# Loading k and v as bf16 by the transfer itself, from GpSimd's queue, in an attention and squared-ReLU kernel on one Trainium2 core

## The chip, the core and the metric

The kernel runs on one core of a Trainium2 chip. A core has TensorE (PE, matrix products), VectorE (DVE), ScalarE (ACT), GpSimd (POOL) and SyncE (SP, which here only issues transfers), and 16 DMA engines that all transfers share. A transfer is issued by an engine's instruction stream: in this kernel SP, POOL and, in three places at the start and one at the end, ACT. Each stream is worked off in its own order, so an instruction that waits holds up what stands behind it on that engine.

The metric is the time of one execution on the device in microseconds (us), median of several runs. A profiled execution gives the trace; its span is the time from the first to the last instruction that the profile shows.

## The reference

Eight batches of eight heads, 576 tokens, head size 64, and 16 extra "beacon" keys and values that every token sees. Causal attention, then a two-layer product with a squared ReLU:

```python
k_all = np.concatenate([beacon_k, k], axis=2)
v_all = np.concatenate([beacon_v, v], axis=2)
scores = scale * np.matmul(q, k_all.transpose(0, 1, 3, 2))
causal[:, Nb:] = np.triu(np.ones((S, S), dtype=bool), k=1)
scores = np.where(causal, -1000000000.0, scores)
a = np.exp(scores - scores.max(-1, keepdims=True))
a /= a.sum(-1, keepdims=True) + 1e-09
attn = np.matmul(a, v_all)
x = np.ascontiguousarray(attn.transpose(0, 2, 1, 3)).reshape(B * S, H * D)   # 4608 x 512
h = x @ w_in                                                                  # 4608 x 2048
r = np.maximum(h, 0.0)
out = (r * r) @ w_out                                                         # 4608 x 512
```

All inputs and the output are float32 in device memory (HBM); the kernel's matrix products take bf16.

## The kernel before

**Attention.** The 592 keys of a batch (16 beacon, 576 own) are cut into five tiles of 128 rows, the last of 80. Scores are made transposed, keys on the partitions, queries along the row: a matmul takes 64 rows of `kT` (one head) as weights and streams `qT` (line 709). ACT takes the exponential into `pt` (line 817), DVE masks the diagonal (839), PE multiplies with `vb` (861), whose 65th column of ones gives the sum of the row, and DVE divides into `xn` (879, 881). `xn` is transposed into `xT`, by PE for batches 0 to 2 (line 930) and by DMA transposes from SP for the later ones (line 913).

**The product layers.** Tokens go in nine chunks of 512. The first layer (line 1174, for the last two chunks 1048) leaves its result in PSUM, ACT or DVE apply ReLU and square (1190 to 1202), and the second layer (1225 for the first chunk, 1288 for the others) multiplies with `w_out`, in a form with seven products in place of eight that needs sums on DVE (`sum_area`, line 1259). `osb` goes to the output.

**How q, k and v come in.** For batches 0 and 1, q and k are loaded in a strided form and transposed by PE (lines 527 and 596, then 559 and 562). From batch 2 on, k and q are loaded by SP, in float32, into one of six staging buffers `stg` (`add_load`, lines 434 to 439), POOL casts each to bf16 in `qk_area` (line 391), and when all five tiles of k, or the five parts of q, are there, SP issues a DMA transpose into `kT` (line 472) or two into `qT` (479, 482). v goes the same way into `vb`, without a transpose; for batches 0 and 1 POOL issues v's loads, after that SP. A k or v tile is eight pieces of 64 float32 (256 bytes) per row, one for each head, and tile 0 has a small extra transfer for the beacons. q is packed, so that a partition reads four tokens (1 KB) at once, but for the first 64 tokens of each head. `kb`, the bf16 form of k in `qk_area`, lies by head pairs, then tiles; so does `kT`.

A load needs a free staging buffer, and the buffer comes free with the cast. There are two copies each of `kb`, `qb`, `kT`, `qT` and `vb`, used by batches in turn: the cast of k waits until the transpose of batch b-2 is done, the cast of v until the attention of b-2 is. v's loads stand behind the issue of the same batch's transposes (`behind`, line 1389).

**What sets the order.** All instructions are registered as operations with an engine, an estimated duration, a priority, dependencies and buffers taken and given back; the class `Order` plays them through once when the program is built, and each engine's instructions are emitted in the order that comes out. `NUDGE` adds to the priorities of single operations, `HOME` fixes the engine where two are possible. `behind` keeps an issue order, `sync` makes an operation wait for another's end though it needs no data from it. Transfers of one issuing engine use eight semaphores in turn: a transfer's issue waits for the eighth one before it to land.

The weights are loaded by POOL, cast to bf16 on the way (`w_in` line 956, `w_out` line 964), in four parts each; SP's first load for batch 2 waits for the last part of `w_out` (`sync`, line 1385).

Of the kernel before, what the change touches and what calls it, by code (L numbers as in the profile page):

```python
# [17 lines left out]
    "tp0.0.0k": 303.651, "ek0.0.2": 3.595, "eq0.0.2": -114.892, "tp0.0.3q": -625.983, "tp0.1.0q": -1223.21,  # L18
    "tp0.1.1k": -824.389, "tp0.1.1q": -1236.66, "tp0.1.3q": -293.65, "qk0.1.2": 199.004, "qk1.0.0": 617.234,
    "av1.0.0": 1322.97, "qk1.1.1": -99.218, "qk3.1.1": 160.424, "tpb1": 1048.34, "tp1.0.1q": -111.345,  # L20
    "av4.0.0": 99785.9, "qk5.7": 99599.4, "exp5.7.0.0.0": 0.67, "qk7.13": 99392, "exp7.13.1.0.0": -47.842,
    "av7.0.0": 100066.370, "xtp1.0.0": 100463.971, "sq0.1.0": 208.303, "s1.0.2.1": 120.167, "s1.0.11.1": 336.481,
    "s1.0.5.1": 124.485, "s1.0.6.0": 71.868, "s1.0.13.0": 41.267, "s2.0.0.0": 56.582, "s2.0.1.0": -99691.1,
    "s2.0.1.2": -20.164, "st0": 41.41, "s2.0.2.1": 690.82, "s2.0.3.0": -109.423, "s2.0.3.1": -11.019,
    "s1.1.0.0": 44.191, "s1.1.8.0": 172.315, "sq1.4.0": -18.208, "s1.1.11.0": 265.496, "s1.1.6.0": 21.125,
    "s1.1.7.0": 229.509, "relu1.7.0": -405.788, "s1.1.14.0": 202.878, "s1.1.15.0": 500.257, "relu1.15.0": 61.707,
    "sum1.3.0": 1108.42, "ev1.u2.None": -82.041, "s2.1.5.1": -100238.506, "s2.1.4.1": -100250.303, "st2": 71.853,
    "tr2q": -203.512, "ld2v1": 28.104, "qk8.2": 100211.101, "exp8.2.1.0.0": -71.878, "qk9.7": 100144.007,
    "exp9.7.-1.0.0": 613.641, "exp9.7.-1.1.0": -8.39, "exp9.7.1.1.3": 182.463, "av9.0.0": 100352.010,
    "exp10.10.-1.1.0": -136.856, "exp10.10.0.0.0": -77.132, "exp10.10.1.0.0": -81.198, "mask10.0.0": -1407.66,  # L30
    "mask10.0.1": -100.11, "mask10.0.2": -199.111, "av10.0.1": 100284.953, "xte2.0.0": 0.336, "xtp2.0.2": 1453.06,
    "sq2.0.0": -147.071, "s1.2.3.0": -101055.411, "relu2.8.0": 93.279, "s1.2.10.0": -63.379, "s1.2.11.0": 583.95,
    "s1.2.4.0": -101060.421, "s1.2.5.0": -289.582, "s1.2.6.0": 23.584, "s1.2.7.0": 55.54, "s1.2.13.0": 20.328,
    "s2.2.2.0": -79.04, "s2.2.2.1": 66.099, "s2.2.6.1": -100314.663, "ev2.u2.None": 280.652, "ev2.c21.None": 433.942,
    "tr3qh": 97.18, "qk12.2": 100532.120, "av12.0.0": 101401.751, "av13.0.1": 101286.864, "exp14.11.1.0.0": 42.246,
    "av14.0.0": 100786.006, "xt3.0": -3.244, "xt3.1": -8.867, "xt3.3": 359.559, "xt3.4": 141.761,
    "s1.3.0.0": -101287.044, "s1.3.2.0": -88.641, "s1.3.8.0": -144.116, "s1.3.9.0": -101292.034, "s1.3.11.0": 912.185,
    "s1.3.5.0": 197.731, "relu3.5.0": -0.786, "s1.3.6.0": -20.095, "sq3.6.0": -5.491, "relu3.15.0": 57.142,
    "sum3.1.1": 1346.77, "s2.3.1.1": 105.485, "ev3.c1.None": 2252.87, "s2.3.5.0": 207.684, "s2.3.7.1": -101083.342,
    "s2.3.4.1": 115.307, "exp16.5.0.0.0": -133.173, "av18.0.0": 101606.833, "av19.0.0": 101753.541,  # L40
    "norm19.0.1": -1613.43, "xt4.0": 111.84, "xt4.3": 195.866, "xt4.4": 195.876, "s1.4.0.0": 931.962,
    "s1.4.1.0": 29.835, "s1.4.2.0": 11.266, "relu4.8.0": 45.602, "s1.4.9.0": -999.566, "sq4.4.0": 10.238,
    "s1.4.11.0": 91.505, "s1.4.6.0": 1005.57, "s1.4.12.0": -942.138, "s2.4.1.0": -12.509, "s2.4.4.0": 1155.18,
    "ld5k1": 217.137, "tr5q": -230.794, "exp20.5.0.0.0": 50.236, "qk21.8": -389.395, "exp21.8.-1.1.0": -59.523,
    "av21.0.0": 101166.223, "av21.0.1": -102.59, "exp22.11.1.0.0": 116.231, "xt5.0": 65.062, "xt5.2": 165.327,
    "xt5.3": 165.337, "s1.5.0.0": 118.705, "relu5.0.0": 45.886, "sq5.0.0": 21.556, "s1.5.2.0": -102472.597,
    "s1.5.3.0": -102569.183, "sq5.1.0": -113.507, "s1.5.8.0": -102706.946, "s1.5.10.0": -907.562,
    "s1.5.11.0": -908.572, "s1.5.4.0": -918, "relu5.4.0": -222.554, "s1.5.5.0": -4.327, "s1.5.6.0": -102580.170,
    "s1.5.7.0": -51.547, "s1.5.12.0": -7.182, "relu5.12.0": -140.259, "sq5.6.0": -436.745, "s2.5.1.0": -83.039,
    "s2.5.2.0": -117.659, "s2.5.5.0": 380.959, "ev5.u3.None": 40.167, "s2.5.4.1": 916.305, "ld6k0": 39.806,  # L50
# [25 lines left out]
    "relu5.12.0": "ACT", "sq5.6.0": "DVE", "ev5.u3.None": "ACT", "sq6.1.0": "ACT", "sq6.5.0": "ACT",  # L76
    "relu6.15.0": "ACT", "ev6.c1.None": "ACT", "ev6.c21.None": "ACT", "h7.0.c1": "ACT", "sq7.0.01": "ACT",
    "sq7.0.10": "ACT", "relu7.1.10": "ACT", "sq8.0.00": "ACT", "sq8.0.10": "ACT", "sq8.0.11": "ACT", "h8.1.u3": "ACT",
    "relu8.1.10": "DVE",
}  # L80


# [168 lines left out]
def kernel(  # L251
# [11 lines left out]
    nc = tc.nc  # L263
    B, H, S, D = q.shape
# [1181 lines left out]
```

## Time and profile before

| | |
|---|---|
| median of 3 runs | 330.49 us (328.14 to 330.75) |
| the profiled execution | 331.13 us, of which its span is 329.4 us |
| mean granted TensorE clock of it | 0.993 |
| HBM read, written | 37.22 MB, 9.44 MB |
| packets of all queues | 125827, of which 106586 under 512 bytes |

The busiest groups of the engines beside PE: the exponentials on ACT (line 817) 71.2 and 23.3 us, ReLU on ACT (1190) 45.6, the masks on DVE (839) 36.9, and on POOL the casts of q and k (391, `qk_area<-stg`) 40.9 us for 60 of them and of v (`vb<-stg`) 28.6 us for 38.

How to read it: a page of the profile gives busy time, share of the span and number of instructions by engine; then the span in 40 slices of 8.2 us, each digit the busy share in tenths, with the clock that the throttle granted TensorE and the busy share of the DMA engines (where packets overlap in time, this share can pass 1 in a stretch). A line of a group reads: source line, engine, operation, written tile <- read tile, count | busy us, mean ns of one | idle time of the engine before them and what ended it. A line of a wait reads: who, for whom: us in total, times, longest. In a table of windows each engine has its busy time and (xinstructions), in the order PE, PEld (weight loads), DVE, ACT, POOL, then the granted clock, the DMA share and GB/s, which count the bytes as written. "SPq" is SP issuing a transfer, "landing" the end of a transfer counted from its issue. Queue 1 is what SP issues, queue 0 what POOL issues, queue 10 what ACT issues.

### The profile page before, as it was taken

The page shows a single profiled execution, that of the slowest core. Times are in us where ns is not written, and L with a number is a line of the kernel's source. Part 1 is how long each engine was busy: PE and PEld are TensorE (multiplying, and loading weights), DVE is VectorE, ACT ScalarE, POOL GpSimd, SP SyncE. Part 2 cuts the span into 40 slices and gives each one's busy share as a digit, 9 for nine tenths or more (in the row PEclk, how much of TensorE's full clock was granted, in tenths as well). Part 3 has the DMA queues.
Part 4 walks back from the last instruction along what each step waited for, and adds up shares of the span by engine and source line. Part 5 has one row for each costly group of instructions (what it writes and reads, how often), then busy time and mean ns, then how long its engine had stood idle before and what let it go on. Part 6 is the DMA issues. An engine that isn't in the chain of part 4 may idle for free.

```text
span 329.4 us, 8951 instructions
## 1 busy us (share of the span) xinstructions
PE 312.8 (95%) x3660; PEld 233.1 (71%) x3678; DVE 237.9 (72%) x490; ACT 235.5 (71%) x352; POOL 101.0 (31%) x147
## 2 busy tenths in 40 slices
PE   2999999989999999999799999999999999999995
PEld 1578865645786468888577545775788788888884
DVE  3888765847985877586937768577955698896871
ACT  3896977469757886787664868688777664879831
POOL 9935703404704614223234105620220260000000
PEclk9999999999999999999799999999999999999999
DMA  9999998999999999499979959987900240020032
GB/s 169 219 207 218 205 152 227 138 254 209 207 198 227 266 181 224 107 236 155 200 177 202 252 95 191 250 164 140 200 5 0 57 146 0 19 112 1 31 130 98
DMA packets 125827, 51.61 MB, mean 157 GB/s; under 512 B 106586, under 2 KB 120794, under 8 KB 125786
## 3 DMA queue, kind: packets, MB, share of 16 engines
q1 hardware_dynamic: 116125, 41.92, 58.5%
q0 software_dynamic: 8512, 8.49, 15.2%
q10 hardware_dynamic: 1149, 0.62, 0.8%
q8 instruction: 29, 0.48, 0.6%
q14 instruction: 12, 0.10, 0.1%
HBM read 37.22 MB, written 9.44 MB: 142 GB/s over the span
## 4 chain that ended last, share of the span: by engine, by line
PE 56%; DMA 21%; DVE 7%; SPq 6%; POOL 5%; ACT 3%; issue 2%; POOLq 0%; DVEq 0%
PE ps L1288 22%; PE ps L1174 15%; PE ps L861 6%; DMA qk_area<-in_q_dram 5%; DMA stg<-in_k_dram 4%; DMA w_out<-in_moe_w_out_dram 4%; PE strip L1048 3%; PE strip L709 3%; DVE sum_area L1259 3%; PE ps L1048 3%; DMA stg<-in_q_dram 3%; SPq L439 2%; PE strip L1288 2%; DMA w_in<-in_moe_w_in_dram 2%; DMA kT<-qk_area 2%
## 5 line engine op out<-in xcount | busy, mean ns | idle before, releaser
L1174 PE MATMUL ps<-xT,w_in 128*128 128x512 bf16 (+6 forms) x626 | 104.7, 314 | 0.7
L817 ACT ACTIVATE pt<-strip 128x1024 bf16<-128x1024 f32 (+3 forms) x89 | 71.2, 851 | 18.3 <-PE strip L709 11.1
L1174 PEld LDWEIGHTS <-w_in 128*128 128x128 bf16 x640 | 57.2, 98 | 34.2 <-issue 1.4
L1190 ACT ACTIVATE g<-ps 128x512 bf16<-128x512 f32 (+2 forms) x85 | 45.6, 539 | 23.3 <-PE ps L1174 22.1
L391 POOL CAST qk_area<-stg 128x512 bf16<-128x512 f32 (+2 forms) x60 | 40.9, 693 | 52.5 <-DMA stg<-in_k_dram 35.3
L1288 PEld LDWEIGHTS <-g 128*128 128x128 bf16 x512 | 48.9, 99 | 8.9 <-issue 2.0
L391 POOL CAST vb<-stg 128x512 bf16<-128x512 f32 (+1 forms) x38 | 28.6, 766 | 84.2 <-DMA stg<-in_v_dram 47.5
L839 DVE TENSOR_TENSOR pt<-pt,tri 128x512 bf16<-128x512 bf16 (+1 forms) x93 | 36.9, 421 | 15.4 <-ACT pt L817 15.1
L1288 PE MATMUL ps<-w_out,g 128*128 128x256 bf16 x352 | 45.9, 277 | 0.0
L1288 PEld LDWEIGHTS <-sum_area 128*128 128x128 bf16 x384 | 36.3, 98 | 7.2 <-DVE sum_area L1259 1.6
L861 PEld LDWEIGHTS <-pt 128*128 128x128 bf16 x930 | 34.9, 98 | 6.6 <-issue 1.0
L861 PE MATMUL ps<-vb,pt 128*128 128x65 bf16 x930 | 37.9, 194 | 0.2
L1192 DVE TENSOR_SCALAR g<-ps 128x512 bf16<-128x512 f32 (+2 forms) x43 | 27.1, 630 | 9.5 <-PE ps L1174 8.2
L881 DVE TENSOR_TENSOR xn<-ps,rcp 128x320 bf16<-128x320 f32 (+2 forms) x64 | 31.5, 492 | 2.4 <-DVE rcp L879 0.2
L1288 PE MATMUL ps<-w_sum,sum_area 128*128 128x256 bf16 x240 | 30.9, 273 | 1.2 <-DVE sum_area L1259 1.0
L709 PEld LDWEIGHTS <-kT 64*128 64x128 bf16 x666 | 21.1, 96 | 15.2 <-issue 8.0
L1200 ACT ACTIVATE g<-g 128x1024 bf16<-128x1024 bf16 (+2 forms) x30 | 29.4, 983 | 1.9 <-DVE g L1192 1.3
L709 PE MATMUL strip<-qT,kT 64*128 64x64 bf16 (+14 forms) x548 | 29.3, 238 | 1.3 <-DMA kT<-qk_area 0.8
L1202 DVE TENSOR_TENSOR g<-g 128x1024 bf16<-128x1024 bf16 (+2 forms) x34 | 22.1, 652 | 11.3 <-ACT g L1190 10.9
L817 ACT ACTIVATE pt<-ps 128x512 bf16<-128x512 f32 x42 | 23.3, 599 | 9.1 <-PE ps L709 5.1
L879 DVE RECIPROCAL rcp<-ps 128x5 f32<-128x5 f32 (+2 forms) x64 | 12.1, 190 | 19.0 <-PE ps L861 17.9
L1312 DVE TENSOR_TENSOR osb<-ps,osb 128x512 f32<-128x512 f32 (+1 forms) x26 | 16.8, 647 | 12.2 <-PE ps L1288 6.4
(91 smaller groups left out, 366.3 us busy)
## 6 DMA issues: line engine op xcount, KB each, us to landing
out_dram<-osb SPq DMA_DIRECT2D x16, 512.0 KB, 3.5
stg<-in_q_dram SPq DMA_DIRECT2D x24, 256.0 KB, 4.5
stg<-in_k_dram SPq DMA_DIRECT2D x18, 256.0 KB, 5.3
stg<-in_v_dram SPq DMA_DIRECT2D x18, 256.0 KB, 5.0
w_in<-in_moe_w_in_dram POOLq DMA_DIRECT2D x4, 512.0 KB, 11.5
w_out<-in_moe_w_out_dram POOLq DMA_DIRECT2D x4, 512.0 KB, 11.2
stg<-in_v_dram POOLq DMA_DIRECT2D x6, 256.0 KB, 8.0
stg<-in_k_dram SPq DMA_DIRECT2D x6, 224.0 KB, 3.8
```

The costliest lines, as they stand in the source:

```text
L391: eng[e].tensor_copy(dst, src)
L709: nc.tensor.matmul(st[hj][:, at + lo:at + hi], kT[b % 2][64 * hj:64 * hj + 64, pr, 128 * c:128 * c + 128], rhs, start=True, stop=True)
L817: nc.scalar.activation(out, in_, AF.Exp, bias=0.0, scale=scale)
L839: nc.vector.tensor_tensor(out=d, in0=d, in1=tri[0:rows, m0:m0 + m, 0:w][:, None].to_broadcast([rows, 2, m, w]), op=ALU.min)
L861: nc.tensor.matmul(a[:, at + (t - tl[0]) * (D + 1):at + (t - tl[0] + 1) * (D + 1)], P[0:rr, hj, o:o + 128], vb[b % 2][0:rr, c, 2 * pr + hj ...
L881: nc.vector.tensor_tensor(out=xn[b % 2].rearrange("p t (h d) -> p h t d", d=D)[:, h0:h0 + nh, tl[0]:tl[0] + nt], in0=a[:, :, :, 0:D], in1= ...
L1174: nc.tensor.matmul(h[:, lo - spans[0][0]:hi - spans[0][0]], w_in_sb[:, mc, ft * 128:(ft + 1) * 128], xT[:, mc, lo % RING:lo % RING + hi - lo],
L1190: nc.scalar.activation(dst, h, AF.Relu, bias=0.0, scale=1.0)
L1192: nc.vector.tensor_scalar(out=dst, in0=h, scalar1=0.0, scalar2=None, op0=ALU.max)
L1200: nc.scalar.activation(d, d, AF.Square, bias=0.0, scale=1.0)
L1202: nc.vector.tensor_tensor(out=d, in0=d, in1=d, op=ALU.mult)
L1288: nc.tensor.matmul(o, lhs[:, f, t * 128:(t + 1) * 128], rhs[:, f], start=fresh and f == 0, stop=f == HF - 1, skip_group_check=True)
```

## The change

- `add_load` serves q alone and issues from SP only. A new `add_direct` loads k of batches 2 to 7 and v of all batches: POOL issues a transfer that reads float32 and writes bf16 straight into `kb` or `vb`. No staging buffer, no cast on POOL (nor the two casts of v on DVE in batch 0).
- A k or v load now itself waits for what the cast waited for: v of batch b for the attention of b-2, k for the transpose of b-2 (in batches 2 and 3 for a memset of the last tile). These loads stand in one chain of issue on POOL.
- `kb` and, from batch 2 on, `kT` lie by tiles, then head pairs (`kT_tile`).
- v's loads no longer stand behind the transposes; in batches 2 and 3 their first one waits until q's transposes have landed, and k's first load of batch 3 until k's transpose of batch 2 has.
- The planner's estimates for the transposes and for transfers from POOL are changed, and `NUDGE` and `HOME` are new throughout, so that the order on every engine differs. The matrix products are the same 3,678 with the same shapes. On SP, k's transpose of batch 2 now comes ahead of q's.

```diff
-    DMA_LAT = {"SP": 0.6, "ACT": 0.6, "POOL": 2.0}
+    DMA_LAT = {"SP": 0.6, "ACT": 0.6, "POOL": 1.1}
...
-    kb = [qk_area[:, (2 * i + 1) * W:(2 * i + 2) * W].rearrange("p (g c d) -> p g c d", g=HP, c=NT)
+    kb = [qk_area[:, (2 * i + 1) * W:(2 * i + 2) * W].rearrange("p (c e) -> p c e", c=NT)
...
+    kT_tile = [kT[i].rearrange("p g t -> p (g t)").rearrange("p (c g t) -> p c g t", c=NT, g=HP) for i in range(2)]
...
+    def add_direct(b, x, c, prio, behind=[], sync=[]):
+        t, beacon = src[x]
+        lo = Nb if c == 0 else 0
+        t0, rows = t_start(c), rows_of(c)
+
+        def emit(e):
+            dst = vb[b % 2][:, c, :, 0:D] if x == "v" else kb[b % 2][:, c].rearrange("p (h d) -> p h d", h=H)
+            insts = []
+            if lo:
+                insts.append(nc.gpsimd.dma_start(out=dst[0:Nb], in_=beacon[b].transpose([1, 0, 2])))
+            insts.append(nc.gpsimd.dma_start(out=dst[lo:rows], in_=t[b, :, t0:t0 + rows - lo, :].transpose([1, 0, 2])))
+            return insts
+
+        deps = []
+        if x == "v" and b >= 2:
+            deps += [o for p in range(HP * (b - 2), HP * (b - 1)) for o in av_ops[p]]
+        if x == "k":
+            deps += [zero_ops[b]] if b < NPE + 2 else trans[b - 2, x]
+        ld = add(f"ld{b}{x}{c}", "POOL", 1.45 if lo else 0.92, emit, prio=prio, deps=deps,
+                 dma=(1.2 if b == 0 else 1.1 if b < NPE else 1.05) * rows / 128, behind=direct_chain[-1:] + behind, sync=sync)
+        direct_chain.append(ld)
+        cast[b, x, c] = ld
...
     def add_load(b, x, c, prio, behind=[], sync=[]):
+        if x != "q":
+            return add_direct(b, x, c, prio, behind, sync)
...
-        soft = b <= 1
-        queue = nc.gpsimd if soft else nc.sync
...
-            if x == "v":
-                copy_on(e, vb[b % 2][0:rows, c, :, 0:D], st[0:rows])
...
-                out=kT[b % 2].rearrange("p g (c t) -> p (g c) t", c=NT),
-                in_=kb[b % 2].rearrange("p g c d -> p (g c d)"),
+                out=kT_tile[b % 2].rearrange("p c g t -> p (c g) t"),
+                in_=kb[b % 2].rearrange("p c e -> p (c e)"),
...
-            elif b == 2 and n == 0:
+            elif b == 2 and x == "q" and c == 0:
                 sync = [w_ops["out", 3]]
             elif b >= NPE and x == "v" and c == 0:
                 for y in "qk":
                     add_trans(b, y, lp - 5.0)
-                behind = trans[b, "q"] + trans[b, "k"]
+                if b in (2, 3):
+                    sync = trans[b, "q"][1:]
+            elif b in (3,) and x == "k" and c == 0:
+                sync = trans[b - 1, "k"]
```

## The prediction

> **What bounds the kernel now.** I read the totals and slices first, then who made TensorE (PE) wait, then windows of 1 us around the longest wait, then the chain of waits, then the groups and the DMA queues.
>
> ```profile
> span 329.4 us, 8951 instructions
> ...
> PE 312.8 (95%) x3660; PEld 233.1 (71%) x3678; DVE 237.9 (72%) x490; ACT 235.5 (71%) x352; POOL 101.0 (31%) x147
> ...
> PE   2999999989999999999799999999999999999995
> ...
> PEclk9999999999999999999799999999999999999999
> DMA  9999998999999999499979959987900240020032
> ```
> PE is the bound: idle for 329.4 - 312.8 = 16.6 us. The 10-us windows put 6.45 us of it before 10 us (3.55 busy) and 3.9 after the last matmul (325.5); 6.3 us lie between. The DMA engines are full until about 240 us: they are the second bound.
>
> ```profile
> PE ps L709 <- DMA kT<-qk_area: 2.0, 1, 2.0
> ...
> PE ps L1288 <- DVE sum_area L1259: 1.0, 2, 0.8
> PE strip L709 <- DMA kT<-qk_area: 0.8, 1, 0.8
> PE ps L709 <- DVE osb L1312: 0.5, 1, 0.5
> ```
> Of PE's waits after 10 us the largest are for a transposed k: 0.8 us before batch 2's scores (at 69.7), 2.0 before batch 5's (at 161.0).
>
> ```profile
> 159.00:160.00 1.00, 0.00 (x0) 0.00 (x0) 0.97 (x3) 0.18 (x1) 0.00 (x0) 1.00 0.51 113
> ...
> 161.00:162.00 1.00, 1.00 (x22) 0.83 (x22) 1.00 (x3) 0.36 (x1) 0.00 (x0) 0.50 1.08 208
> 162.00:163.00 1.00, 1.00 (x11) 0.44 (x4) 1.00 (x2) 1.00 (x4) 0.45 (x1) 0.50 1.07 209
> 163.00:164.00 1.00, 1.00 (x7) 0.74 (x5) 1.00 (x2) 1.00 (x5) 1.00 (x2) 0.50 1.21 241
> 164.00:165.00 1.00, 1.00 (x9) 0.81 (x8) 1.00 (x2) 0.75 (x1) 1.00 (x2) 0.80 1.15 104
> ```
> The third column from the end is the granted clock. Behind the 2.0-us wait it falls to 0.50, which costs 3 x 0.5 + 0.2 = 1.7 us of work counted as busy.
>
> ```profile
> 56.92 6.15 DMA stg<-in_k_dram
> 63.20 1.62 POOL qk_area L391
> 64.83 3.10 SPq L472
> ```
> The chain shows why k is late: load into staging, GpSimd (POOL) cast, then the transpose's issue, all of it in one SP queue.
>
> **The change, part by part.** *PE's work* is the same 3,678 matmuls with the same columns; the tile layout changes only addresses. The transposes move the same 20 blocks of 128x128, so I leave them at 3.1 us of issue and 5.7 to landing.
>
> *POOL.* Removed: 38 v casts (28.6 us), 24 full k casts x 0.661 + the six of 80 rows (5.5) = 21.4; together 50.0. Added: 12 batches' worth of issues (k and v of 2 to 7), each 0.55 + 5 x 0.865 = 4.87, 58.5 us (v of 0 and 1 was issued there already). 101 becomes about 110 of 329 us. *SP* loses 72 issues, some 43 us at a median of 0.4 to 0.85. *VectorE (DVE)* loses two v casts (0.9). POOL and SP are idle most of the time, so none of this is on the path by its sum; it matters by what it queues.
>
> ```profile
> L439 POOL DMA_DIRECT2D stg<-in_v_dram x10 | 8.6, 865 | 6.1 <-DVE xn L881 1.9 <-DVE g L1192 1.9 <-DMA w_in<-in_moe_w_in_dram 1.2
> ```
> ```profile
> q1 hardware_dynamic: 116125, 41.92, 58.5%
> q0 software_dynamic: 8512, 8.49, 15.2%
> ```
> *The DMA engines.* No row shows a cast transfer with 256-byte reads and 128-byte writes. Bounds: the cast of w_out writes 204 to 208 GB/s (41 to 46 us), 131 KB in 0.64 us; the present v loads, also 256-byte pieces, run at 208 to 250 GB/s (124 to 128 us, mean 224), 262 KB in 1.17 us. A tile costs 0.64 to 1.17. I take 0.9, near the middle: the engine work per piece is that of the second row, the bytes written that of the first. Queue 1 now holds 58.5% of 329.4 = 193 us, all queues 248. 12 x 4.63 = 55.5 tiles leave queue 1 (65 us) and enter queue 0 at 36 to 65, 50 at my value: 248 becomes 219 to 248, 233 at my value. In the first 240 us, where the engines are now full, that is room for the late k.
>
> *Batch 2* is the tight place, and the new order asks more of it. I counted matmul columns (at least 64 each) at 2.4 per ns (in the chain eight of 256 take 0.87 us, 2.35 per ns). The old order puts 58.3 us of PE work ahead of batch 2's scores, and PE reached them at 68.9: an offset of 10.6. The new one puts 53.2 ahead, so PE arrives at 63.8. What can be there: w_out landed at 49.2, with the DMA share at 0.48, 0.12, 0.00, 0.20 from 47 to 51, because SP's loads wait for that landing. The new k loads wait on POOL for no such thing (only for the eighth transfer before), and follow w_out directly: 4.63 x 0.64 to 1.17 puts them at 51 to 54. k's transpose is issued until 57; q shares the engines, lands about 57, its last POOL cast ends at 58, its two transposes take 2.8 + 1.4 of SP and 2.3 to land: 64.5. So a stall of 0 to 1.5, I take 0.5 (before: 0.8).
>
> v2 is the next tight one: its issue waits for q2's transposes (64.5), takes 4.9, and lands 3.9 to 6.2 later (SP's v loads now), 73 to 76, against 66.5 + 10.6 = 77.1. I cost it at nothing; each us beyond that would be a us of PE.
>
> *Later batches.* v loads of batch b wait on POOL for the attention of b-2, and q casts and k loads of b+1 queue behind them. With the same offset: v4 waits until 84.8 + 10.6 = 95, k5 behind it lands near 107 and is wanted at 136.4 + 10.6 = 147; v5 waits until 134, k6 lands near 147, wanted at 180; v6 waits until 165, wanted at 190; k7 and v7 have 30 us or more. Those waits are covered, so batch 5's 2.0 us and its 1.7 of clock go, and nothing of this path is next.
>
> *DVE's share.* The 0.8 and 0.5 us around 88 and 91 (sum_area, osb) come through a chain from v's landing (79.2) over its cast, the attention and its normalization. With v earlier they shrink, but all of DVE's order is new: I take 0.6 of 1.3, bounds 0 and 1.3. The head, the tail and the last 90 us (PE idle 0.3 in 240 to 320) stay.
>
> Sum, against the profiled run's own 331.13 (span 329.4 and 1.73 around it): -0.8 + 0.5 - 2.0 - 1.7 - 0.6 = -4.6, so 326.5. That run was 0.64 above the median of 330.49 and just above the highest timed one (330.75); a run of 328.14 exists, perhaps without the clock dip. Against the median 326.5 is -1.2%.
>
> **A rule against the change.** A DMA issued on POOL has its pieces written by POOL, beside a busy DVE. In the trace those issues took 0.74 to 1.03 us between 6 and 31 us, with DVE 73 to 93% busy; POOL casts, though, stretched from 0.61 to 1.94. The Trainium skill, "SBUF — State Buffer", "SBUF: two separate sides", says that a DVE instruction in a two-port mode locks GpSimd out of writing descriptors, so such a DMA starves, and advises the SP or ACT queue. The 0.74 to 1.03 us agree only weakly with that; the mechanism is priced as the fourth rival.
>
> **Rivals.**
> 1. *All middle idle goes*: 331.13 - 6.3 - 1.7 + 0.5 = 323.6. For it: a free DMA lets every engine run ahead. Against: 2.3 us of that idle has no DMA behind it. Chance 0.10.
> 2. *The clock dips anyway* behind some shorter gap: 326.5 + 1.7 = 328.2. For it: a gap of only 2.0 us was enough here. The Trainium skill, "TensorE: Matmul & The Clock Gate", Part 1, ties the half clock to an idle window of some 3.4 us; by that the 2.0-us gap would not explain this dip, which could then come back. The dip beginning right at the gap's end speaks for my reading. 0.12.
> 3. *The wait changes hands*: ACT and DVE (71 and 72%) get a new order, and what k gave up comes back as waits on them, or the loads were hidden but for 2.8 us that runs without the dip lack: 329 to 332, middle 330. 0.12.
> 4. *DVE holds up POOL's issues*: at the cast's stretch (1.94/0.61 = 3.2) six issues take 6 x 0.865 x 3.2 = 16.6 us; from 41 on, k2 is ready at 57.6 instead of 54, a stall of about 4 with its clock dip: 326.5 + 3.6 + 1.7 = 331.8. Against it: the issue rows. 0.04.
> 5. *Slower: the 128-byte writes cost more than the 256-byte pieces did.* Above 1.17 us a tile the engines have more to do than now, when they are full and just fit. At 1.6, 55.5 x 0.43 = 24 us extra before 240 us; k2 is 2 us later, and if half of the excess shows the time is about 343, all of it 355. Nothing shows such writes; against it, casts with long pieces lose nothing per byte read. 0.14.
>
> **How the numbers follow.** My case has 0.48 (own range 324.5 to 328.5: the tile cost, batch 2's 0 to 1.5, DVE's 0 to 1.3). One per cent, 3.3 us, is about what can be told apart, so "faster" means below 327.2, "slower" above 333.8. Faster: 0.36 of my 0.48, rival 1's 0.10, 0.02 of rival 2: 0.48. Slower: rival 5 (0.14) and 0.02 of 3: 0.16. The rest, 0.36, is the same. The range 323 to 332 holds my case and rivals 1 to 4, and leaves rival 5 out.
>
> **What would show it.** Right: no PE wait for kT above 1 us; granted clock 1.00 after the start; queue 1 near 39%, queue 0 between 26 and 35%; POOL issues of 0.8 to 1.0 us; batch 2's scores near 64 us. Wrong: a wait for kT or vb in the new path, queue 0 well over 35%, POOL issues of 2 us and more, or the same PE idle with ACT or DVE as releasers. A slowdown with kT on time would throw over the whole reading.

## The result, and the profile after

The changed kernel takes 342.95 us (median of 4 runs, 339.60 to 343.25) against 329.31 us for the kernel before on the same chip (4 runs): a ratio of 1.0391, 95% interval 1.0304 to 1.0477. It is 4% slower. The prediction was 326.5 us with a range of 323 to 332, and it was wrong in sign. The profiled execution took 343.13 us. Ratios and their intervals leave disturbed runs out and medians do not, so in the table further down the two can differ by up to half a per cent.

The page's totals and slices, in the same lines as shown of before:

```profile
span 341.3 us, 8841 instructions
...
PE 316.3 (93%) x3661; PEld 234.5 (69%) x3678; DVE 232.7 (68%) x498; ACT 226.7 (66%) x342; POOL 105.0 (31%) x151
...
PE   1999999994999997968999999999999999999996
...
PEclk9999999998999999995999999999999999999999
DMA  9999999799999999899139999801310060030033
```
PE is idle for 341.3 - 316.3 = 25.0 us where it was 16.6 before, and its busy time grew by 3.5 us. Of these, 2.2 are half clock: it lasts 10.2 us here (82.4 to 85.8 and 154.1 to 160.9), and PE worked in 7.8 of them, which costs 3.9 us; before it was 1.7. The DMA engines are first empty in slice 27 (222 us) and not in 30 (239 us) as before, so their work is done earlier, and it bought nothing. The damage lies in slices 10 (78 us), 16 to 19, and in the two dents of the clock.

What PE waited for:

```profile
PE ps L561 <- ACT qk_area L391: 6.3, 2, 4.3
PE ps L864 <- DMA vb<-in_v_dram: 5.0, 2, 3.7
PE strip L713 <- ACT pt L820: 2.6, 4, 1.1
PE ps L1177 <- DMA xT<-xn: 1.7, 1, 1.7
PE ps L1291 <- DVE osb L393: 1.4, 2, 0.8
PE ps L864 <- DVE pt L842: 1.3, 2, 0.7
```
No wait for a transposed k (`kT<-qk_area`) is left: that is what the change was forecast to do, and it did it. In its place stand two new waits for transfers (`vb` 5.0 us, `xT` 1.7) and 5.3 us of short waits for ACT and DVE (rows three, five and six). The first line is the start of the kernel, 0.9 us more idle time there than before.

The first stop in windows of 1 us (columns as before: PE, PEld, DVE, ACT, POOL, clock, DMA share, GB/s):

```profile
78.00:79.00 1.00, 0.00 (x0) 0.00 (x0) 0.75 (x2) 0.53 (x1) 1.00 (x2) 1.00 1.57 216
79.00:80.00 1.00, 0.00 (x0) 0.00 (x0) 0.00 (x0) 0.00 (x0) 0.67 (x2) 1.00 2.05 111
...
82.00:83.00 1.00, 0.00 (x0) 0.00 (x0) 0.00 (x0) 0.00 (x0) 0.00 (x0) 0.69 1.61 157
83.00:84.00 1.00, 0.88 (x4) 0.33 (x4) 0.60 (x2) 0.00 (x0) 0.00 (x0) 0.50 1.60 160
```
PE, and soon every engine, stands still while the DMA engines are full: v of batch 2 is not there. Its last tile was issued at 68.04 and landed at 83.08. The clock is halved from 82.4 us on.

The second stop, in the chain of waits (start, us, what):

```profile
145.04 1.32 SPq L916
...
147.90 8.74 DMA xT<-xn
...
156.69 2.95 PE ps L1177 x12
```
The five transposes of batch 3's attention into `xT` need 8.7 us to land (their median; 2.5 before). At the same moment POOL issues v of batch 5 and, behind it, k of batch 6 (144.4 to 155.8 us): the transposes and v of batch 5 were set free by the same event, the end of batch 3's attention.

The second dent of the clock does not begin with this stop, though; the stop only prolongs it. It begins at 154.07, and PE runs out of `xT` at 155.0:

```profile
152.00:153.00 1.00, 0.13 (x4) 0.12 (x5) 0.54 (x2) 0.82 (x1) 1.00 (x2) 1.00 3.57 116
...
154.00:155.00 1.00, 1.00 (x14) 0.62 (x10) 0.93 (x4) 1.00 (x4) 0.00 (x0) 0.53 0.99 77
155.00:156.00 1.00, 0.01 (x1) 0.00 (x0) 0.81 (x3) 0.55 (x2) 0.93 (x2) 0.50 1.69 229
```
Ahead of it, from 147.5 to 152.9 us, PE waited four times for ACT and DVE (0.5, 0.6, 0.5 and 1.1 us) in a stretch of scores and attention products alone.

POOL's issues of v, and the two queues:

```profile
L430 POOL DMA_DIRECT2D vb<-in_v_dram x40 | 33.6, 854 | 7.4 <-DMA w_in<-in_moe_w_in_dram 6.0 <-DMA qk_area<-in_k_dram 0.8 <-DMA qk_area<-in_q_dram 0.3
```
```profile
q0 software_dynamic: 75328, 14.56, 56.0%
q1 hardware_dynamic: 58141, 27.37, 40.5%
```
The issues cost 0.854 us each, as forecast. Queue 0's 56.0%, well over the forecast's 35, can't be read as a price: packets that overlap are each counted in full (E4's first casts, alone in their stretch, read 149.7%). The fastest of the versions below (E14) has 66.7% there.

### The profile page after: what moved, and what is told of

Same layout as the page of the kernel before. It is cut to its first block, busy times and chain, and to the rows that moved or that the text cites. A ratio compares the mean times of both kernels' runs of the same rounds, so it can differ in the third digit from the quotient of the medians.

```text
span 341.3 us, 8841 instructions
## 1 busy us (share of the span) xinstructions
PE 316.3 (93%) x3661; PEld 234.5 (69%) x3678; DVE 232.7 (68%) x498; ACT 226.7 (66%) x342; POOL 105.0 (31%) x151
## 4 chain that ended last, share of the span: by engine, by line
PE 64%; DMA 22%; POOL 4%; DVE 4%; SPq 2%; ACT 2%; issue 2%; POOLq 0%; ACTq 0%; DVEq 0%
PE ps L1291 23%; PE ps L1177 22%; DMA vb<-in_v_dram 6%; PE ps L864 6%; DMA qk_area<-in_q_dram 5%; DMA w_out<-in_moe_w_out_dram 4%; PE strip L1051 4%; PE strip L713 3%; PE ps L1051 3%; DMA xT<-xn 3%; PE strip L1291 2%; DMA qT<-qk_area 2%; POOL vb L430 2%; DMA stg<-in_q_dram 2%; ACT pt L820 1%
## 5 line engine op out<-in xcount | busy, mean ns | idle before, releaser
L1177 PE MATMUL ps<-xT,w_in 128*128 128x512 bf16 (+6 forms) x627 | 107.9, 320 | 2.5 <-DMA xT<-xn 1.7
L820 ACT ACTIVATE pt<-strip 128x1024 bf16<-128x1024 f32 (+4 forms) x89 | 70.9, 850 | 8.4 <-PE strip L713 4.8
L1193 ACT ACTIVATE g<-ps 128x512 bf16<-128x512 f32 (+2 forms) x80 | 43.9, 554 | 38.4 <-PE ps L1177 37.2
L842 DVE TENSOR_TENSOR pt<-pt,tri 128x512 bf16<-128x512 bf16 (+1 forms) x93 | 32.4, 374 | 20.5 <-ACT pt L820 20.0
L1291 PE MATMUL ps<-w_out,g 128*128 128x256 bf16 x352 | 43.7, 273 | 0.8 <-DVE osb L393 0.8
L430 POOL DMA_DIRECT2D vb<-in_v_dram x40 | 33.6, 854 | 7.4 <-DMA w_in<-in_moe_w_in_dram 6.0
L713 PE MATMUL strip<-qT,kT 64*128 64x64 bf16 (+17 forms) x548 | 29.2, 234 | 2.9 <-ACT pt L820 2.6
L393 POOL CAST qk_area<-stg 128x512 bf16<-128x512 f32 (+1 forms) x30 | 19.3, 658 | 33.0 <-DMA stg<-in_q_dram 24.4
L391 ACT COPY osb<-ps 128x512 f32<-128x512 f32 x23 | 13.5, 586 | 23.2 <-PE ps L1291 14.1
L1205 DVE TENSOR_TENSOR g<-g 128x1024 bf16<-128x1024 bf16 (+2 forms) x33 | 20.3, 622 | 12.4 <-ACT g L1193 11.9
## 6 DMA issues: line engine op xcount, KB each, us to landing
qk_area<-in_k_dram POOLq DMA_DIRECT2D x18, 128.0 KB, 11.1
w_out<-in_moe_w_out_dram POOLq DMA_DIRECT2D x4, 512.0 KB, 10.4
```

The source lines that it names most:

```text
L430: insts.append(nc.gpsimd.dma_start(out=dst[lo:rows], in_=t[b, :, t0:t0 + rows - lo, :].transpose([1, 0, 2])))
L713: nc.tensor.matmul(st[hj][:, at + lo:at + hi], keys, rhs, start=True, stop=True)
L820: nc.scalar.activation(out, in_, AF.Exp, bias=0.0, scale=scale)
L842: nc.vector.tensor_tensor(out=d, in0=d, in1=tri[0:rows, m0:m0 + m, 0:w][:, None].to_broadcast([rows, 2, m, w]), op=ALU.min)
L1177: nc.tensor.matmul(h[:, lo - spans[0][0]:hi - spans[0][0]], w_in_sb[:, mc, ft * 128:(ft + 1) * 128], xT[:, mc, lo % RING:lo % RING + hi - lo],
L1193: nc.scalar.activation(dst, h, AF.Relu, bias=0.0, scale=1.0)
```

## The experiments

Three theories stood after the comparison of the traces. **A, the pieces:** a cast load in 128-byte pieces keeps the DMA engines as long as the staged load did, so nothing is relieved. **B, the two queues:** what POOL issues no longer stands in line with SP's transposes and q loads but beside them, and both become late. **C, the order:** the new order of PE, ACT and DVE is worse by itself.

All medians in us; the kernel before has 329.1 to 329.8 in the calls they come from.

| | kernel | median | ratio to before, 95% interval |
|---|---|---|---|
| - | changed | 342.95 | 1.0391, 1.0304 to 1.0477 |
| E1 | changed, k and v in rows of 2 KB | 340.73 | 1.0350, 1.0278 to 1.0423 |
| E2 | before, k and v in rows of 2 KB | 329.93 | 1.0004, 0.9968 to 1.0041 |
| E3 | changed, two waits | 341.33 | 1.0385, 1.0297 to 1.0474 |
| E5 | changed, few loads | 335.62 | 1.0187, 1.0146 to 1.0228 |
| E6 | before, few loads | 329.43 | 1.0002, 0.9963 to 1.0042 |
| E7 | E1 and one wait | 334.43 | 1.0152, 1.0115 to 1.0189 |
| E8 | before, tables of the changed | 337.68 | 1.0265, 1.0215 to 1.0316 |
| E9 | changed, one table entry out | 331.82 | 1.0075, 1.0037 to 1.0114 |
| E10 | E9 and two waits | 330.74 | 1.0017, 0.9981 to 1.0054 |
| E11 | changed, planned anew | 334.28 | 1.0123, 1.0055 to 1.0192 |
| E12 | E11, q of batch 4 behind v of 2 | 344.05 | 1.0405, 1.0316 to 1.0494 |
| E13 | E9, few loads | 325.92 | 0.9901, 0.9867 to 0.9935 |
| E14 | E9, v of batch 2 early | 326.76 | 0.9918, 0.9884 to 0.9952 |
| E15 | E9, q of batch 4 held | 328.54 | 0.9982, 0.9947 to 1.0017 |
| E16 | E14 and E15 | 329.91 | 0.9974, 0.9927 to 1.0021 |
| E17 | changed, v of batch 2 early | 339.35 | 1.0283, 1.0206 to 1.0361 |
| E18 | E17 and the wait of E7 | 337.59 | 1.0198, 1.0112 to 1.0284 |

Line numbers in the rows below are those of each experiment's own file, up to 15 above the changed kernel's.

### E1, E2: an eighth of the pieces

```diff
+            flat = t[b].rearrange("h s d -> (h s d)").rearrange("(r e) -> r e", e=H * D)[t0:t0 + rows - lo]
+            if b >= 2:
+                whole = vb[b % 2].rearrange("p c h d -> p c (h d)")[:, c, 0:H * D] if x == "v" else kb[b % 2][:, c]
+                insts.append(nc.gpsimd.dma_start(out=whole[lo:rows], in_=flat))
+                return insts
```


> The changed kernel, same order on every engine and same queues, but the loads of k and v of batches 2 to 7 read contiguous rows of 2 KB instead of eight pieces of 256 bytes: the same bytes in an eighth of the pieces. k and v of these batches therefore hold other tokens, and v overwrites its column of ones; all engine work keeps its shape. Theory A (the pieces: a cast load keeps the DMA engines as long as the staged load did, about 1.2 us a tile, so nothing is relieved): with the pieces gone the time falls to 326 to 330 us and the PE waits for vb at 78 and for xT at 156 vanish. Theory B (the two queues: loads on GpSimd's queue are served beside SP's transposes and q loads instead of before or behind them): shorter loads disturb less, also 326 to 332. Theory C (the order: the new order of ACT's, DVE's and PE's work is worse by itself, whatever the DMAs do): 338 or more.

> The kernel before, with the staged loads of k and v of batches 2 to 7 reading contiguous rows of 2 KB (they hold other tokens; casts, order and queues stay). It shows what relieved DMA engines are worth to the order of before. Theory A: the PE waits for kT at 69.7 and 161.0 and the clock dip go, 326 to 328 us against 329.3. Theory B and C: much the same, 326 to 329; if the loads were hidden but for SP's own issue time, no change at all (329).

E1 came out at 340.73, far from 326 to 330, and E2 changed nothing (329.93). In E1's table of PE waits `vb` is gone, but:

```profile
PE ps L1182 <- DMA xT<-xn: 5.8, 1, 5.8
PE strip L718 <- ACT pt L825: 2.6, 4, 1.1
```
The wait for `xT` grew from 1.7 to 5.8 us: PE comes to it 5 us earlier, since the first stop is gone, and the transposes land after 11.4 us (median) instead of 8.7. The half clock there lasts 13.65 us; it begins at 147.5 us, ahead of this wait (150.0 to 155.9), behind the same stretch of short waits. Theory A's forecast is wrong. Theory B's is wrong too as stated (326 to 332), though the grown wait is its mechanism. Theory C's (338 or more) holds. The 2.6 us for ACT are untouched.

### E3: two waits, no order changed

```diff
+LATER = {"ld3q3": ["ld2v4"], "ld5v0": ["xt3.3", "xt3.4"]}
...
+                for f in LATER.get(op.name, ()):
+                    self.wait_for(op.insts[0], issued[rank[f]][0].insts[-1])
```


> The changed kernel with two waits added and no order changed: SP's load of the fourth q tile of batch 3 waits until the last v tile of batch 2 has landed, and GpSimd's first load of v of batch 5 waits until the transposes of batch 3's attention (xT) have landed. Not a byte less is moved. Theory B: the v of batch 2 lands near 75 instead of 83 and xT about 4 us earlier, both PE stops (78 to 86, 154 to 161) shrink to under 1 us with their clock dips, 333 to 336 us. Theory A: the engines are as full as before, the lateness only moves to k of batches 3 and 6: 339 to 345. Theory C: 341 to 343.

341.33, with runs from 337.13 to 343.15. In the profiled run, the fastest, both stops are gone from PE's waits, but 7.3 us for ACT, DVE and `kT` remain, all between 95 and 150 us:

```profile
PE strip L726 <- ACT pt L833: 2.6, 4, 1.1
PE ps L877 <- DVE pt L855: 2.0, 2, 1.3
PE ps L1304 <- DVE osb L406: 1.4, 2, 0.8
PE strip L726 <- DMA kT<-qk_area: 1.3, 1, 1.3
```
What separates its runs is mostly the clock: its mean is 0.994 in the run of 337.13 us and 0.979 in the two of 343. Repairing both stops alone wins little as long as PE starves elsewhere and the clock falls there. That was a second sign for C, whose range (341 to 343) the median fits.

### E4: the forms of transfer alone

A kernel of its own, no diff: each section is one of the kernel's forms of transfer and waits for the section before it.

> Not the kernel: each form of transfer alone, eight tiles of 128 rows by 512 numbers in a section, sections kept apart by waits, the output filled with other numbers; its time says nothing. To read: the time from first issue to last landing of each section. Theory A: cast loads with 256-byte reads and 128-byte writes take 1.1 to 1.3 us a tile, as much as the uncast ones on either queue, and rows of 2 KB 0.5 to 0.9. If the cast loads take 1.6 or more, my fifth rival was right in its mechanism; if 0.9, the theory falls. Theory B: two transposes of 20 blocks take about 8 us alone and 14 or more when eight cast loads start on the other queue at the same moment, while the packed q loads beside casts land as late as the casts.

The timeline (start, us, what, and the idle time before it with its releaser); in each pair of rows the first is the issue of eight tiles and the second the first instruction that waited for their landing:

```profile
31.03 7.15 POOL L59 DMA_DIRECT2D kb<-in_k_dram  x8 [30.58 <-DVE zero L41]
41.75 0.17 DVE L42 CAST zero<-kb 128x8 f32<-128x8 bf16 x1 [10.90 <-DMA kb<-in_k_dram]
42.40 7.01 POOL L59 DMA_DIRECT2D vb<-in_v_dram  x8 [4.23 <-DVE zero L42]
54.09 0.17 DVE L43 CAST zero<-vb 128x8 f32<-128x8 bf16 x1 [11.77 <-DMA vb<-in_v_dram]
...
54.67 7.02 POOL L59 DMA_DIRECT2D st<-in_v_dram  x8 [5.26 <-DVE zero L44]
66.93 0.15 DVE L40 COPY flag<-st 128x1 f32<-128x1 f32 x1 [12.56 <-DMA st<-in_v_dram]
...
68.06 4.29 POOL L59 DMA_DIRECT2D kb<-in_k_dram  x8 [6.37 <-DVE zero L41]
76.97 0.17 DVE L42 CAST zero<-kb 128x8 f32<-128x8 bf16 x1 [9.09 <-DMA kb<-in_k_dram]
```
Eight cast tiles take 10.7 us for k and 11.7 for v, eight uncast ones 12.3, eight in rows of 2 KB 8.9. In the trace the tiles land 1.01, 1.12, 1.20 and 0.85 us apart. So a cast saves 13% of the uncast load's time for k and 5% for v, and an eighth of the pieces saves another 17% for k: E1 relieved less than theory A assumed. The views of the DMA issues in three sections (count, KB each, median us from issue to landing) are two transposes alone, two beside eight cast loads on POOL's queue, and two behind eight loads in SP's own queue:

```profile
kT<-zbt SPq DMA_TRANSPOSE x2, 5.1
...
kb<-in_k_dram POOLq DMA_DIRECT2D x8, 128.0 KB, 9.8
kT<-zbt SPq DMA_TRANSPOSE x2, 10.4
...
st<-in_k_dram SPq DMA_DIRECT2D x8, 256.0 KB, 4.9
kT<-zbt SPq DMA_TRANSPOSE x2, 5.6
```
Theory B's mechanism is shown here by itself: beside the casts a transpose needs 10.4 us instead of 5.1, and the casts 9.8 instead of 4.4. Side by side the whole takes 17.0 us, where the casts alone take 10.7 and the two transposes alone 8.2: the engines have hardly less to do, and both are late. In line it takes 17.1 us, but those eight loads are uncast (SP's), so this is not quite the same work; there the loads and the transposes keep about their own times (4.9 and 5.6 us).

### E5, E6: an eighth of k's and v's traffic

```diff
+            if b >= 3 or b == 2 and x == "v":
+                return [nc.gpsimd.dma_start(out=dst[0:16], in_=t[b, :, t0:t0 + 16, :].transpose([1, 0, 2]))]
```


> The changed kernel, where each load of v of batch 2 and of k and v of batches 3 to 7 brings 16 rows of a tile instead of 112 to 128: an eighth of the bytes and of the pieces, same queues, same order, one issue for each tile. The other rows of k and v keep what stood there (zeros in batch 3's k, set by one larger memset on GpSimd), all engine work keeps its shape. It takes these loads off the DMA engines and so off every other transfer. Theories A and B (the loads' transfers, by their amount or by disturbing transposes and q): 325 to 330 us, with no DMA among PE's waits after 40 us. Theory C (the order of PE, ACT and DVE by itself): the waits for ACT and DVE between 120 and 150 us and their clock dips stay, 334 or more.

> The same in the kernel before: staged loads of v of batch 2 and of k and v of batches 3 to 7 bring 16 rows instead of 112 to 128; casts stay whole, with old data in the other rows. It is the partner of the run above: the difference of the two is what the two orders are worth without the load traffic. Theories A and B: 325 to 329, within 1% of the changed kernel treated so. Theory C: 5 us or more below it.

335.62 against 329.43. The edit takes 11.5 of the 37.2 MB read, and q's loads stay. Theory C forecast this pair: with so little of k and v moved, the changed kernel is still 6.2 us behind the old one (the pair differs in the form of the loads too; E13 below doesn't). PE's timeline in E5 (start, us, what, and the idle time before it with its releaser):

```profile
141.54 0.40 PE L715 MATMUL strip<-qT,kT 64*128 64x192 bf16 x4 [0.48 <-ACT pt L822]
141.87 0.33 PE L866 MATMUL ps<-vb,pt 128*128 128x65 bf16 x5
142.83 0.94 PE L866 MATMUL ps<-vb,pt 128*128 128x65 bf16 x25 [0.63 <-DVE pt L844]
143.70 0.70 PE L715 MATMUL ps<-qT,kT 64*128 64x144 bf16 x6
144.94 0.41 PE L715 MATMUL strip<-qT,kT 64*128 64x176 bf16 x10 [0.53 <-ACT pt L822]
147.30 0.61 PE L715 MATMUL strip<-qT,kT 64*128 64x112 bf16 x6 [1.96 <-ACT pt L822]
147.84 1.83 PE L866 MATMUL ps<-vb,pt 128*128 128x65 bf16 x30
149.49 0.83 PE L1179 MATMUL ps<-xT,w_in 128*128 128x192 bf16 x4
```
From 140.4 to 149.5 us PE has only scores (715) and attention products (866). The second layer of one chunk has ended, and the first layer of the next needs `xT` of batch 3. With nothing in between, scores wait for exponentials and a product for the mask, 3.6 us in all: bare attention. E6 says something else as well: the kernel before gains nothing (329.43) when most of the traffic of k and v is taken away. Those transfers were hidden, and the 4.5 us of waits and half clock that I had found in one profiled run were not in its median: of 87 later executions of that kernel 72 have a mean clock of 0.997 or more, the profiled one 0.993.

### E7, E8: one wait with the rows, and the tables alone

E7 is E1 with the second entry of E3's table; E8 exchanges `NUDGE` and `HOME` as wholes.

> The changed kernel with k and v of batches 2 to 7 read as contiguous rows of 2 KB (other tokens) and, besides, GpSimd's first load of v of batch 5 waiting until the transposes of batch 3's attention (xT) have landed. Reading rows alone took away the wait for vb at 78 us but made the one for xT longer (5.8 us and a half clock for about 10 us behind it). Theory B (two queues served side by side): with the wait that stop goes too and some 9 to 12 us with it, 329 to 332. Theory A: no more than 2 us below reading rows alone, since the rows had relieved the engines already. Theory C: 335 or more, from the waits for ACT and DVE at 120 to 150.

> The kernel before with its own staged loads, but with the tables of the changed kernel that nudge and place the work (the two tables at the head of the file, exchanged whole; entries for steps that do not exist here do nothing). It shows the tables without the loads they came with. Theory C: slower by as much as the change was, 337 or more, with waits for ACT and DVE. Theories A and B: within 2 us or so of the kernel before in what the order itself costs, 329 to 334, though tables that do not fit their loads may cost some more.

E7 at 334.43 is as good as E5 with its little traffic, 6.3 us below E1: there the collision at `xT` was worth that. The rest, 5 us above before, has the waits that C named (2.6 for ACT, 1.5 and 1.4 for DVE); the time falls between the bounds of B and C. E8 at 337.68 is 8.3 us slower with the old loads; its stops lie elsewhere (2.4 us for `xn` at 68 us), so it shows that these tables don't fit the old loads, not that the same fault is in them.

### E9, E10: one entry of the table

```diff
-    "s2.0.3.3": -45.347, "s1.1.1.0": 705.342, "s1.1.3.0": 79.121, "s1.1.8.0": 70.066, "s1.1.9.0": 68.338,
+    "s2.0.3.3": -45.347, "s1.1.1.0": 705.342, "s1.1.8.0": 70.066, "s1.1.9.0": 68.338,
```
(The number is a priority, not a time as the expectation says.)

> The changed kernel with a single entry taken from the table that nudges the order (a step of the first product of the second block of 512 tokens, 79 ns later than its base); the planner then lays out the work from about 85 us on anew, attention of batches 3 and 4 spread among products again, with the same loads on the same queues. Theory C (about 6 of the 13.6 us are the order's, the bare attention at 120 to 150 us): the waits for ACT and DVE there shrink from 6.7 us to 2 or less, and the time falls to 334 to 338. If the whole loss came from the loads (A and B): 341 to 344, the stops only moving.

> The same, with two waits added and no order changed: SP's load of the fourth q tile of batch 3 waits for the last v tile of batch 2, and GpSimd's first load of v of batch 5 waits for the first three transposes of batch 3's attention (xT). Theory B together with C (order 6 us, disturbed transfers 7 us): 328 to 332, no PE wait for vb at 78 and none for xT above 0.5 us. If the waits do nothing beyond the order, as they did little alone (341.3): within 1 us of the kernel without them.

E9 takes 331.82: one entry is worth 11.1 of the 13.6 us, more than theory C forecast. The planner picks greedily, so a shifted priority lays out all later work anew; here products stand between the parts of the attention again, PE is idle for 0.0 us between 120 and 150 (4.2 in the changed kernel, 6.2 in E5). The loads of batch 5 still meet batch 3's transposes, which land after 5.8 to 8.0 us, but PE has other work meanwhile and never waits for `xT`. The stop at 78 us is still there (3.6 us for `vb`, and a half clock). E10 removes it, but holds SP back, and in its only trace, an execution of 334.81 us, k of batch 3 is late:

```profile
PE strip L726 <- DMA kT<-qk_area: 7.1, 1, 7.1
```
There the lateness moved; what the faster executions wait for is not known. The median of 330.74 can't be told from E9's, since the intervals overlap.

### E11, E12: planned anew

The planner lets the two queues share the engines, counts 1.2 us for a cast tile (1.05 before), and has tables found on that planner alone. E12 has in addition:

```diff
+            elif b == 4 and x == "q" and c == 0:
+                sync = [cast[2, "v", NT - 1]]
```


> The changed kernel with the same loads, whose planner shares the DMA engines between the two queues (a load on GpSimd's queue slows one on SP's and the other way round, where the planner had put all in one line), prices a cast load at 1.2 us a tile, and has new tables, found on that planner alone. No bare attention is left in the order. Theory B and C together (the loads are neither better nor worse than the old ones, what was lost was the order and the meeting of the two queues): no wait of PE for a DMA above 1.5 us and none for ACT or DVE above 1 us after 10 us, 326 to 331. If the direct loads cost time by themselves, whatever the order (theory A): still 331 or more, as with the single entry.

> The same again, where besides the q loads of batch 4 wait until the v of batch 2 has landed (v2 was the last late transfer, with q and k of later batches beside it), and the tables are found for that. Theory B: v of batch 2 is there in time, PE idle between 10 and 320 us below 3 us, 325 to 330, perhaps a little under the kernel before. If that wait only moves the lateness to k of batch 3 (as the two waits did, 7.1 us at 96): 331 or more.

Both miss the range of theories B and C and lie in the other one, 331 or more. That the loads cost this in any order does not follow: E14 below carries the same loads in 326.76 us. E11 has no single wait for a transfer above 0.5 us, but 334.28 us: PE is busy 3.6 us longer than in E14 (315.4 against 311.8; 1.7 of it a half clock behind a wait of 2.2 us for DVE at 272), and idle in many small pieces. E12 has 344.05, with stops of 5.1 us for `xT` at 177 and 4.3 us of issue at 207. A better model of the DMA engines in the planner did not find a better kernel; why E12's two stops arise was not followed.

### E13 to E16: what the loads cost in the mended order

E13 is E9 with the edit of E5. E14 takes one wait away, E15 adds one and moves a cast on POOL, E16 does both:

```diff
+FREE = ("ld2v0",)
+LATER = {"ld4q0": ["ld2v4"]}
...
-                for d in op.sync:
+                for d in op.sync if op.name not in FREE else []:
...
+        issued.insert(at["ld3k4"], issued.pop(at["cast4q0"]))
```


> The changed kernel without the one table entry, and with the loads of v of batch 2 and of k and v of batches 3 to 7 bringing 16 rows of a tile instead of 112 to 128 (the other rows hold what stood there). It shows what the load traffic costs in the mended order. If the late v of batch 2 is all of it: 325 to 327.5, that is 4 to 6 us below the run with full loads, and below the kernel before treated so (329.4). If the direct loads cost nothing there: 330 to 332.

> Without the one entry, all loads in full; the first load of v of batch 2 no longer waits for q2's transpose (its place on GpSimd's queue stays, behind the first q cast of batch 3), which lets it be issued about 4 us earlier. If its own late issue is the cause: v2 lands near 79, PE's stop at 78 falls from 3.6 us to below 1, no half clock, 326 to 329. If the neighbours on SP's queue are: it lands above 81 all the same, or q2's transposes land later and batch 2's scores wait 1 to 2 us: 330 to 333.

> Without the one entry, all loads in full; SP's first load of q of batch 4 waits until the last v tile of batch 2 has landed, and its cast on GpSimd stands behind the loads of k of batch 3 instead of ahead of them. If the neighbours are the cause: v2 lands near 79, the stop falls below 1.5 us, 327 to 329. If its own late issue is: the stop stays above 2.5 us, 330 to 333. If the wait only moves the lateness: a wait for kT or qT of batch 3 near 95 instead.

> Both edits of the two runs above together. With either cause v2 should then be in time and 325 to 328.5 come out, below the kernel before (329.4); if it stays at 330 or more, the direct loads do not pay even where no PE wait names them.

E13 takes 325.92. Beside E5, with the same form of loads and as little traffic, it prices the order: 335.62 - 325.92 = 9.7 us for one entry. Beside E9 it prices the loads: 331.82 - 325.92 = 5.9 us. E14 gets 5.1 of these back with all its loads: v of batch 2, issued from 60.3 instead of 64.7 on, lands its last tile at 73.6 instead of 81.6 (E9). Its page:

```profile
span 325.0 us, 8837 instructions
...
PE   2999999999999999999999999999999999999995
...
PEclk9999999999999999999999999999999999999999
```
No dent, no half clock, and 326.76 us, 0.8% faster than the kernel before (interval 0.5 to 1.2%). It is the one version with all its loads whose interval lies below the kernel before. Here too batch 3's first transposes are late (6.8 to 9.2 us to landing), and PE waits 0.3 us for them. Holding q of batch 4 back (E15) mends the stop too: v's last tile lands at 75.6, so q beside it was a cause of its lateness. PE then waits 1.8 us for `kT` (1.6 in E14), and 328.54 can't be told from before. Both together (E16) make k of batch 3 late again (3.5 us at 97) and lose most of the gain.

### E17, E18: the stops mended, the entry kept

> The changed kernel with its whole table, where only the first load of v of batch 2 no longer waits for q2's transpose. If the two causes add: the stop at 78 to 83 us (5 us) and its half clock (1.7) go, the rest stays, 336 to 338. If the bare attention and the second stop swallow what is won, as with the two waits (341.3): 340 to 343.

> The same, and GpSimd's first load of v of batch 5 waits for the transposes of batch 3's attention (xT). Both stops for a DMA are then mended and only the order is left: by the run with few loads (335.6) I expect 335 to 338 with waits for ACT and DVE at 120 to 150 and one or two half clocks there; 330 or less would speak against the order as a cause of its own.

339.35 and 337.59, the second within its range (335 to 338). The freed v2 is worth 3.6 us with the entry and 5.1 without. E18's wait is worth another 1.8 us by the medians, though with executions from 335.30 to 340.60 that is not certain (the traced one, of 340.60, has a new wait of 3.5 us for `kT` at 97). With both stops mended the changed order stays 10.8 us above E14, close to the 9.7 of the pair without traffic. E17 falls between its two forecasts (336 to 338, 340 to 343): it has no wait for a transfer above 0.7 us left, yet half clock lasts from 146.5 to 156.7 us, over the bare attention.

**What is settled.** In the changed kernel the order costs 6.2 us against the old one (E5, E6) and 9.7 against its own mended form (E5, E13). The transfers of the loads cost 7.3 more (342.95 - 335.62), by lateness of two things that share the engines with them, v of batch 2 and `xT` of batch 3; mending both gave 5.4 of it back (E18). The second lateness needs the order as well: in E9 and E14 the transposes are as late, and PE hardly waits. With one entry out and v2 early, the change is worth 0.8% (E14). That gain is hardly the lighter traffic, of which the kernel before makes nothing (E6), and E13 stands 3.5 us below E6: it lies in the mended order, or in the casts and issues that POOL and SP no longer do. These two were not separated. Open is also why E3's runs scatter over 6 us, since only its fastest left a trace.

## Why the prediction was wrong, step by step

The prediction's last sign came true: a slowdown with `kT` on time, which was to throw over the whole reading.

- **Batch 2's scores near 64 us, no wait for k: right.** They ran at 64.87 without a wait for `kT`.
- **POOL's issues at 0.865 us: right** (0.854 for v). The fourth rival falls: the issues were not stretched, beside a DVE that is busy for 68% of the span. The rule of the Trainium skill behind it, "SBUF — State Buffer", "SBUF: two separate sides", that a DVE instruction in a two-port mode starves such transfers, shows in no run here.
- **A tile at 0.9 us: mis-sized,** 1.01 (k) to 1.12 (v) alone, inside the bounds. On 55.5 tiles that is 6 to 12 us of engine time. It did not decide: with tiles at 0.85 (E1) the kernel was 2 us faster, no more. The fifth rival named 343 us, but its price of 1.6 us a tile is not there: that its number came out is luck.
- **"A stall of 0 to 1.5" for -0.8, and "batch 5's 2.0 us and its 1.7 of clock go": the waits went, the gain did not.** They belonged to one execution. Relieved of its loads, the kernel before is no faster (E2, E6). The third rival, at a chance of 0.12, had this in half a sentence (loads "hidden but for 2.8 us that runs without the dip lack"), and the waits on ACT and DVE from a new order in another; its 329 to 332 us was too low.
- **v2 "lands 3.9 to 6.2 later ... I cost it at nothing": this step failed.** The landing times were those of loads in SP's own line. With q of batches 3 and 4 on the other queue v2's last tile took 15.0 us, and 1.1 us of forecast slack (76 against 77.1) became a stop of 5.0 us and 1.3 of half clock. I had added up the engines' work, and never asked who shares them with v2 while it travels.
- **"Those waits are covered ... and nothing of this path is next": this step failed.** I followed the waits of the loads, and not what the loads do to others. Next was `xT`, freed by the same event as v of batch 5, with k of batch 6 behind it: 1.7 us of wait in this order, 5.8 in E1.
- **"All of DVE's order is new: I take 0.6 of 1.3": this step failed by the most.** I let the new order of ACT, DVE and PE be neutral but for 1.3 us, and it costs 6.2 to 9.7 by itself (E5 against E6 and E13). The bare stretch could have been seen: PE's new sequence holds nothing but scores and attention products between the last product of one chunk and the first of the next, while in the trace of before products of the layers stand between them and PE is idle for 0.0 us from 120 to 150.

With the order mended by one entry and one wait removed, the same loads give 326.76 us, next to the forecast's 326.5. That is luck and doesn't save the forecast: it added up waits that were not in the median, and it priced a kernel that was not there.

## What to carry to other kernels

When a change brings a new order with it, price the order first: look along PE's new sequence for stretches without independent work between dependent steps, and along each event for the transfers that it sets free together. Moving loads to another queue doesn't make the DMA engines wider; it takes away the line in which urgent and patient transfers stood, so each pair that can now meet, and whose late half an engine waits for, needs a wait, a head start (E14) or other work to cover it (E9). And take a gain from a wait only if several executions have it.

## What the runs showed of the hardware

**Two queues share the engines: both become late, and little is won in total.** Alone, two transposes land after 5.1 us and eight cast loads after 4.4; side by side it is 10.4 and 9.8, and the whole takes 17.0 us against 10.7 and 8.2 one by one (E4). The Trainium skill, "DMA: Bandwidth & Descriptors", "Queues, rings and completion order", says that each DMA engine takes turns between the queues packet by packet; that both are held up by about as much, 5.3 and 5.4 us, agrees with it (single packets were not followed). Longer pieces on one queue may slow the other's small ones more: `xT` lands after 8.7 us beside 256-byte pieces and after 11.4 beside 2-KB ones, in one trace each (E1).

**The clock follows busy shares of fixed stretches, not the length of a gap.** In the traces' clock records every half-clock period between the start and the end lasts 3.41 us or a multiple of it (6.83, 10.24, 13.65). I cut 19 traces, of before, after and all experiments but E4, into stretches of 3.41 us that fall on these changes (some traces lack a few matmuls). Of the stretches at full clock that end before the last matmul, all 16 in which PE's matmuls were busy for 56% or less were followed by half clock, none with 65% or more was, and in between one of five. At the very end it is otherwise: three stretches with 47 to 53% (E7, E9, E14) had one more at full clock behind them. Back to full clock it took about 80%. In E7 no gap of PE there was longer than 1.1 us:

```profile
144.00:145.00 1.00, 0.56 (x7) 0.28 (x7) 0.30 (x1) 1.00 (x2) 0.00 (x0) 1.00 0.08 9
145.00:146.00 1.00, 0.41 (x10) 0.29 (x10) 0.81 (x3) 0.51 (x2) 0.00 (x0) 1.00 1.00 317
146.00:147.00 1.00, 0.31 (x6) 0.22 (x5) 0.54 (x3) 0.64 (x1) 0.00 (x0) 0.65 1.00 280
147.00:148.00 1.00, 1.00 (x19) 0.77 (x16) 0.25 (x1) 0.66 (x2) 0.00 (x0) 0.50 0.62 122
```
So short waits that add up to 1.5 us within one stretch cost another 1.5 us of clock here. The Trainium skill, "TensorE: Matmul & The Clock Gate", Part 1, ties the half clock to an idle window of some 3.4 us; the window's length agrees, but here it need not be idle, and the measurement decides.
